# A hand-written order and a planner: moving one unit's outputs, the load gates and the order of a stage in a fused attention and feed-forward kernel

## The chip, the cores and the metric

The kernel runs on one core of one Trainium2 chip. The metric is the device time of one execution in microseconds (us). The engines are named as in the profile: PE is TensorE (matmuls), PEld its weight loads, DVE is VectorE, ACT is ScalarE, POOL is GpSimd, SP is SyncE, which here only issues transfers.

## The reference, cut to what matters

A linear attention with decay over 4 batches, 8 heads, 768 positions and head size 64, followed by a feed-forward layer with a "snake" activation:

```python
for b in range(nb):                      # 12 blocks of 64 positions
    intra = (qb @ kb.T * Dmask) @ vb     # per batch and head
    inter = (qb * lam_pow) @ kv_state
    out[block b] = intra + inter
    kv_state = lam_block * kv_state + kb_dec.T @ vb
x = out as [3072 tokens, 512]
h = x @ w_in                             # 512 -> 2048
g = h + sin(alpha * h) ** 2 / (alpha + 1e-9)
return g @ w_out                         # 2048 -> 512
```

## The kernel before

**Attention.** The work is cut into 24 units: unit s holds a batch, a pair of 128-position blocks and half of the heads. `load_x(s)` issues three transfers on SP's queue (q, k and v of the unit, 256 KB each). `prep(s)` calls `scale_block(s)`, which writes q times a power of lambda, k cast to bf16, and v times a power of lambda (L498 for q and v on POOL or DVE, L509 for k on ACT or POOL). `piece_T(s)` transposes q and k: for units below 8 on TensorE into bank 0 with a copy out (L528, L533; "T4" in the order), from unit 8 on by a transposing transfer on SP's queue (L518), which `prep(s)` issues. `run(S, O, Z)` is one block of small matmuls (L603): S stands for the scores of a unit, O for the outputs of a unit whose masked scores are ready, Z for the sum of k times v that the next unit needs. After it come the masking of the scores (M, L623, DVE), the cast of the sum (Z, L632), the copy of the outputs into xT (E, L642, ACT or DVE), and for outputs of units from 4 on a wipe of half of two banks (L649, DVE). `piece_G(s, s - 1)` ("G5") is one run with scores and sum of unit s, and with the outputs of unit s - 1 unless those have already been computed by a run of their own ("O4", "O7", "O8", which enter `ahead`). Inside a run that has matmuls both before and after the scores, the last part waits on a semaphore for the first.

**Feed-forward.** The 3072 tokens are 6 chunks of 512; chunk c needs the outputs of units 4c to 4c + 3. The first layer of a chunk has 16 column blocks m. `unit_A` does one m for all 512 tokens (four matmuls of 512 columns, L673), `unit_A2` two m for half of the tokens (eight matmuls of 256 columns, L707). Behind them ACT computes the sine (t, L683 or L717), ACT or POOL the square (u, L687, L688, L721, L722), DVE the sum into gT (L690, L725). Only then is the bank free. `unit_B` is a quarter of the second layer for 128 tokens (four matmuls, L738), every fourth followed by a copy (L751) and a store (L753). Chunk 0's first layer uses six banks, chunk 1's three (5, 6, 7) in turn.

**Weights.** The quarter 0 of w_in comes over SP (ws, cast at L437), the other three quarters of w_in (w1_1 to w1_3) and the four of w_out (w2_0 to w2_3) over POOL's queue, cast on the way. The string `LOADS` gives their order together with units 4 to 9 (written v_4 to v_9, although all three transfers are meant): "w2_1:v_4" is not issued before v of unit 4 has landed.

**What sets the order.** Every step is first entered into a list with an estimated duration, its reads, its writes and a place. `_Plan._order` then lays the list out in time by those estimates, and each engine's queue is emitted in that order, with semaphore waits for what the estimates got wrong. TensorE may take any of its next 40 entries: the one with the lowest place among those that start within 0.3 us of the earliest. SP keeps the order of the text. ACT, DVE and POOL take what starts first, and where several could start, the lowest place; `lead` moves a place ahead by so many entries. Some steps may go to either of two engines, by the estimates.

**The stage that the change touches.** After units 0 to 3 the kernel does chunk 0's first layer (eight A2, eight A). Then comes the string `FIRST`: "B" is the next quarter of the second layer, "0" and "1" are the next A2 of chunk 1 for its first and second half of tokens, "A" a `unit_A` of chunk 1, P, T, G, O and L are prep, transposes, a run with scores, a run of outputs, and loads of the unit named. The stores of chunk 0 are issued on SP where the sixteenth B stands. After `FIRST` a loop over chunks 2 to 5 alternates A and B with the remaining units, and the last B follow alone.

Of the kernel before, what the change touches and what calls it, by code (L numbers as in the profile page):

```python
# [270 lines left out]
def bass_lightning_attn__then__act_snake_kernel(  # L271
# [10 lines left out]
    B, H, S, D = q.shape  # L282
# [23 lines left out]
    with es:  # L306
# [48 lines left out]
        def _(_unused_eng):  # L355
            P = _Plan(
                {"PE": nc.tensor, "ACT": nc.scalar, "DVE": nc.vector, "POOL": nc.gpsimd, "SP": nc.sync},
                new_sem,
            )
# [20 lines left out]
            def hop(kind, s, eng, *rest, **more):  # L380

                lead, P.lead = P.lead, P.lead + RANK.get((kind, s), 0)
                e = HEAD.get((kind, s))
                o = op(e, rest[0], COST[kind][e], *rest[2:], **more) if e else op(eng, *rest, **more)
                o.port = kind in ("q", "k", "v", "ws") or (kind, s) == ("alpha", 2)
                P.lead = lead
                return o
# [5 lines left out]
            def bank(i):  # L393
                return ("bank", i)
# [39 lines left out]
            def cast_w1_first():  # L434
                for lo in (0, 256):
                    hop("ws", lo // 256, "DVE",
                       lambda e, lo=lo: (e.copy if e is nc.scalar else e.tensor_copy)(  # L437
                           w1[:, :, lo:lo + 256], ws[:, :, lo:lo + 256]), 0.7, [("ws", lo)], [("w1", lo // 256)])
# [99 lines left out]
            def run(S=None, O=None, Z=None, b0=3, obs=None, parted=False, after=(), us=(0, 1)):  # L538
# [3 lines left out]
                first, free, then = [], [], []  # L542
# [49 lines left out]
                busy = {(a, b): 0 for a in range(2) for b in range(2)}  # L592
                first, early, then = [dealt(g, busy) for g in (first, free, then)]
# [16 lines left out]
                reads, writes = [], []  # L610
# [6 lines left out]
                for r, z in sums:  # L617
                    reads += [("k2", z % R2), ("v2", z % R2)]
                    writes += [bank(ZB[z % 2])] * (bank(ZB[z % 2]) not in writes)
                hop("P", (S, O, Z), "PE", mm, (0.17 if first and then else 0.15) + max(busy.values()) / 1000, reads, writes, after=after)  # L620
                lead, P_.lead = P_.lead, -20
                if S is not None:
                    hop("M", (S, us), "DVE", lambda e: e.tensor_tensor(  # L623
# [29 lines left out]
            def piece_G(s, t):  # L653
                run(S=s, O=t, Z=s)
# [107 lines left out]
            def prep(s, more=True):  # L762
                if s < NBLK:
                    if more and 4 < s < NBLK - 2:
                        load_x(s + 2)
                    P.lead = -20 if 3 < s < 15 else 0
                    P.lead = 0 if 3 < s < 15 else 0
                    P.lead = 20 if 3 < s < 15 else 0
                    scale_block(s)
                    P.lead = 0  # L770
                    P.lead = 0
                    P.lead = 0
                    if s >= TD:
                        piece_T(s, None)
# [25 lines left out]
            run(O=3, obs=(6, 7), parted=True)  # L800
            load_w1_first()
            cast_w1_first()
            LOADS = "w1_1:q_3 w1_2:k_3 w1_3:q_3 v_4 w2_0:q_3 w2_1:v_4 v_5:w1_2 w2_2:w1_2 v_6:ws_1 v_7:w1_3 v_8:ws_0 w2_3:w1_2 v_9:w1_3"
            for x in LOADS.split():
                x, _, gate = x.partition(":")
                x, i = x.split("_")
# [32 lines left out]
            def attend(kind, s):  # L839
# [3 lines left out]
                else:  # L843
                    if 12 < s < NBLK:
# [1 line left out]
                    piece_G(s if s < NBLK else None, s - 1 if s > 4 and s - 1 not in ahead else None)  # L846
                P.lead = 0

            FIRST = ("P4 B P5 P6 B T4 B P7 G4 L10 B B B O4 B T5 T6 B "
# [3 lines left out]
            AT = {2: (5, 8, 12, 13), 3: (2, 6, 10, 13), 4: (2, 6, 10, 13)}  # L853
            at = [0, 0]
            ahead = set()
            for x in FIRST.split():
                if x in "01":
# [8 lines left out]
                elif x[0] == "O":  # L866
                    s = int(x[1:])
# [66 lines left out]
```

## Time and profile before

| | |
|---|---|
| three runs | 214.80, 214.88, 215.81 us; median 214.88 |
| the profiled execution, its own time | 214.99 us |
| its span, first to last instruction | 213.2 us |
| granted TensorE clock | 1.00 in every stretch |
| DMA share, 17.6 to 80.1 us | 1.08 to 1.23 (16 engines, overlapping packets count twice) |
| read from HBM, written | 27.27 MB, 6.29 MB |

A row of the timeline has start, length, engine, line, operation, what it writes and reads, and a count where neighbours were merged; in brackets the engine's idle time ahead of it and what ended it. A matmul's length includes its way through the array, so lengths of neighbours overlap, and distances between starts say what a piece costs. A row of a group (line, engine, operation) has the count, then the total busy time and the mean in ns, then idle time ahead.

### The profile page before, as it was taken

The numbers are of one execution on the slowest core, as the hardware profiler recorded it, in microseconds if no ns is written. First come the engines' busy times: TensorE is split into PE (matmuls) and PEld (weight loads), VectorE is DVE, ScalarE is ACT, GpSimd is POOL, SyncE is SP. The second block draws the span as 40 slices with busy tenths as digits, with TensorE's granted clock in tenths as the row PEclk, the third lists the DMA queues.
The fourth block names the chain that finished last, engine by engine and source line by source line (L and its number), as shares of the span: only waits on it lengthen the run. The fifth ranks groups of instructions, "written<-read, shape, count | busy, mean of one in ns | idle before, by whom it ended". The sixth has DMA issues, their size and how long they took to land.

```text
span 213.2 us, 5249 instructions
## 1 busy us (share of the span) xinstructions
PE 202.9 (95%) x2219; PEld 108.8 (51%) x2219; DVE 124.5 (58%) x196; ACT 162.3 (76%) x296; POOL 74.9 (35%) x82
## 2 busy tenths in 40 slices
PE   7577999999999999999999999999999999999995
PEld 3355834556677655455545545445545444444443
DVE  4584589647788896674846557546646544444200
ACT  6487998149998898878978978888888787888421
POOL 3676787167657554884168400000000000000000
PEclk9999999999999999999999999999999999999999
DMA  5999999999999999999999921101101101110122
GB/s 160 291 318 260 207 212 216 270 279 282 189 268 239 267 284 248 203 300 317 228 206 283 177 49 52 49 3 49 52 0 51 52 0 49 51 52 6 43 98 98
DMA packets 63323, 34.43 MB, mean 161 GB/s; under 512 B 18611, under 2 KB 60355, under 8 KB 63299
## 3 DMA queue, kind: packets, MB, share of 16 engines
q1 hardware_dynamic: 56688, 25.24, 52.7%
q0 software_dynamic: 3696, 3.67, 10.3%
q10 hardware_dynamic: 2914, 5.19, 6.6%
q8 instruction: 17, 0.28, 0.6%
q14 instruction: 8, 0.06, 0.1%
HBM read 27.27 MB, written 6.29 MB: 157 GB/s over the span
## 4 chain that ended last, share of the span: by engine, by line
PE 77%; DVE 7%; SPq 4%; ACT 4%; DMA 3%; POOL 3%; issue 1%; ACTq 0%; POOLq 0%
PE bank L738 37%; PE bank L673 27%; PE bank L603 7%; PE bank L707 5%; SPq L397 4%; DMA ws<-in_moe_w_in_dram 3%; DVE gT L725 2%; POOL u L722 2%; ACT t L717 2%; DVE Sm L623 2%; DVE bank L649 1%; PE bank L528 1%; DVE gT L690 1%; DVE xT L642 1%; ACT u L721 0%
## 5 line engine op out<-in xcount | busy, mean ns | idle before, releaser
L738 PE MATMUL bank<-w,gT 128*128 128x512 bf16 (+2 forms) x400 | 95.5, 371 | 0.0
L690 DVE SCALAR_TENSOR_TENSOR gT<-u,rinv,bank 128x512 bf16<-128x512 bf16 x70 | 51.7, 744 | 44.5 <-ACT u L687 40.6
L673 PE MATMUL bank<-xT,w 128*128 128x512 bf16 x280 | 70.7, 379 | 0.1
L683 ACT ACTIVATE t<-bank,alpha 128x512 bf16<-128x512 f32 x70 | 47.7, 688 | 17.4 <-PE bank L673 17.4
L738 PEld LDWEIGHTS bank<-w,gT 128*128 128x128 bf16 x400 | 36.9, 98 | 39.4 <-ACT osb L751 0.9
L673 PEld LDWEIGHTS bank<-xT,w 128*128 128x128 bf16 x280 | 27.1, 98 | 33.1 <-DVE gT L725 1.1
L687 ACT ACTIVATE u<-t 128x512 bf16<-128x512 bf16 x61 | 38.3, 631 | 1.8
L623 DVE TENSOR_TENSOR Sm<-bank,mask 128x1024 bf16<-128x1024 f32 (+1 forms) x25 | 29.3, 1177 | 8.8 <-PE bank L603 8.8
L498 POOL TENSOR_TENSOR qk<-q,Lq 128x512 bf16<-128x512 f32 x24 | 25.3, 1054 | 12.8 <-DMA q<-in_q_dram 10.5
L498 POOL TENSOR_TENSOR v<-v,Lk 128x512 bf16<-128x512 f32 x22 | 22.9, 1042 | 13.3 <-DMA v<-in_v_dram 10.2
L707 PE MATMUL bank<-xT,w 128*128 128x256 bf16 x208 | 25.6, 273 | 1.7 <-ACT w L437 0.5
L725 DVE SCALAR_TENSOR_TENSOR gT<-u,rinv,bank 128x256 bf16<-128x256 bf16 x52 | 21.7, 469 | 7.8 <-POOL u L722 6.3
L717 ACT ACTIVATE t<-bank,alpha 128x256 bf16<-128x256 f32 x52 | 22.2, 473 | 3.7 <-PE bank L707 3.5
L751 ACT COPY osb<-bank 128x512 f32<-128x512 f32 (+2 forms) x25 | 14.0, 562 | 12.0 <-PE bank L738 12.0
L707 PEld LDWEIGHTS bank<-xT,w 128*128 128x128 bf16 x208 | 19.4, 98 | 6.6 <-DVE xT L642 0.9
L509 ACT CAST qk<-k 128x512 bf16<-128x512 f32 x22 | 13.6, 619 | 6.2 <-DMA k<-in_k_dram 6.2
L722 POOL TENSOR_TENSOR u<-t 128x512 bf16<-128x512 bf16 x10 | 10.4, 1040 | 8.9 <-ACT t L717 8.8
L642 ACT CAST xT<-bank 128x512 bf16<-128x512 f32 (+1 forms) x18 | 13.0, 722 | 0.4 <-PE bank L603 0.3
L688 POOL TENSOR_TENSOR u<-t 128x512 bf16<-128x512 bf16 x9 | 9.3, 1039 | 10.0 <-ACT t L683 9.2
L632 ACT CAST Zc<-bank 128x256 bf16<-128x256 f32 x22 | 8.0, 365 | 5.3 <-PE bank L603 5.3
L603 PE MATMUL bank<-qkT,Zc 64*64 64x128 bf16 x160 | 11.4, 228 | 0.5
L649 DVE MEMSET bank<- 128x512 f32 x20 | 9.7, 485 | 3.2 <-ACT xT L642 1.1
(53 smaller groups left out, 111.9 us busy)
## 6 DMA issues: line engine op xcount, KB each, us to landing
q<-in_q_dram SPq DMA_DIRECT2D x24, 256.0 KB, 5.4
k<-in_k_dram SPq DMA_DIRECT2D x24, 256.0 KB, 5.3
v<-in_v_dram SPq DMA_DIRECT2D x24, 256.0 KB, 5.6
out_dram<-osb ACTq DMA_DIRECT2D x19, 256.0 KB, 2.0
w<-in_moe_w_out_dram POOLq DMA_DIRECT2D x4, 512.0 KB, 13.1
w<-in_moe_w_in_dram POOLq DMA_DIRECT2D x3, 512.0 KB, 10.7
ws<-in_moe_w_in_dram SPq DMA_DIRECT2D x2, 512.0 KB, 6.9
out_dram<-osb SPq DMA_DIRECT2D x4, 256.0 KB, 3.5
```

What stands on the lines that cost most here:

```text
L498: return lambda e: e.tensor_tensor(out, bass.AP(x32[x][jl], 0, [[8 * D, 128], [4 * D, 2], [D, 4], [1, D]]), bass.AP(L, (2 * n + g) * 8, [[ ...
L603: ins = e.matmul(d, w, x, start=key not in begun, stop=True, skip_group_check=True)
L623: hop("M", (S, us), "DVE", lambda e: e.tensor_tensor(Sm[S % 2][:, us[0]:us[-1] + 1, :, :].rearrange("p u w i -> p (u w i)").rearrange("p ( ...
L642: hop("E", O if not parted else (O, r0), eng, lambda e, r0=r0, r1=r1, ra=ra, way=way: (e.copy if e is nc.scalar else e.tensor_copy)(bass.A ...
L673: ins = e.matmul(ps[hb][:, c0:c1], w1[:, kc, 128 * m:128 * (m + 1)], xT[x][:, kc, c0:c1], start=(kc == 0 and c0 == lo), stop=(kc == NKC - ...
L683: op("ACT", lambda e: e.activation(t16[ju][:, w], ps[hb][:, w], ACTF.Sin, scale=alpha[:, m:m + 1]), 0.69 * f, [bank(hb), "alpha"], [("t16" ...
L687: lambda e: (e.activation(u16[ju][:, w], t16[ju][:, w], ACTF.Square) if e is nc.scalar else e.tensor_tensor(u16[ju][:, w], t16[ju][:, w], ...
L690: op("DVE", lambda e: e.scalar_tensor_tensor(out=gT[g][:, m, w], in0=u16[ju][:, w], scalar=rinv[:, m:m + 1], in1=ps[hb][:, w], op0=ALU.mul ...
L707: ins = e.matmul(ps[hb][:, 256 * i:256 * i + 256], w1[:, kc, 128 * (m + i):128 * (m + i + 1)], xT[x][:, kc, lo:lo + 256], start=(kc == 0 a ...
L717: op("ACT", lambda e, i=i: e.activation(t16[ju][:, 256 * i:256 * i + 256], ps[hb][:, 256 * i:256 * i + 256], ACTF.Sin, scale=alpha[:, m + ...
L725: op("DVE", lambda e, i=i: e.scalar_tensor_tensor(out=gT[g][:, m + i, lo:lo + 256], in0=u16[ju][:, 256 * i:256 * i + 256], scalar=rinv[:, ...
L738: ins = e.matmul(ps[ob][:, w], gT[g][:, m, 128 * s4:128 * (s4 + 1)], w2[:, m, w], start=(m == 0), stop=(m == NM - 1),)
```

## The change

Five edits, all in what the planner is given:

- the estimated length of a run: 0.17 or 0.15 us plus its matmuls before; now 0.12 for a run with one part, 0.165 where scores stand between the two parts, 0.39 where they don't (O4, O7, O8)
- the lead of `scale_block` for units 4 to 14: from 20 entries ahead to 20 entries back
- `LOADS`: unit 4's loads and w2_0 come first in the text; v_4 is gated on k_3, w2_0 on v_4 (before: q_3), w1_1 on k_3, unit 5 on w1_3 (before: w1_2), units 6 to 9 on other gates, all of which come behind unit 5 on the same queue
- `FIRST`: "O4" is gone, so that G5 computes unit 4's outputs; the rest is ordered anew, with the same count of B, G, P, T and L; the two closing A are one more 0 and one more 1
- in consequence the loads of units 11 and 12 stand one transposing transfer further ahead on SP, and chunk 0's stores behind the loads of units 14 to 16

```diff
-                hop("P", (S, O, Z), "PE", mm, (0.17 if first and then else 0.15) + max(busy.values()) / 1000, reads, writes, after=after)
+                hop("P", (S, O, Z), "PE", mm, (0.12 if not then or not first else 0.165 if early else 0.39) + max(busy.values()) / 1000, reads, writes, after=after)
...
                     P.lead = -20 if 3 < s < 15 else 0
                     P.lead = 0 if 3 < s < 15 else 0
-                    P.lead = 20 if 3 < s < 15 else 0
+                    P.lead = -20 if 3 < s < 15 else 0
                     scale_block(s)
...
-            LOADS = "w1_1:q_3 w1_2:k_3 w1_3:q_3 v_4 w2_0:q_3 w2_1:v_4 v_5:w1_2 w2_2:w1_2 v_6:ws_1 v_7:w1_3 v_8:ws_0 w2_3:w1_2 v_9:w1_3"
+            LOADS = "v_4:k_3 w2_0:v_4 w1_1:k_3 w2_1:v_4 w1_2:q_3 w1_3:q_3 v_5:w1_3 w2_2:w1_2 v_6 v_7:w1_1 v_8:w1_3 w2_3:w1_2 v_9:w2_0"
...
-            FIRST = ("P4 B P5 P6 B T4 B P7 G4 L10 B B B O4 B T5 T6 B "
-                     "P8 B T7 B B B P9 L11 G5 P10 G6 B 0 G7 0 O7 L12 0 "
-                     "0 1 G8 1 O8 B 0 G9 L13 1 1 G10 1 0 1 P11 P12 1 "
-                     "B B G11 P13 0 L14 G12 B L15 L16 B P14 A A")
+            FIRST = ("B P4 P5 P6 B P7 B L10 B T4 T5 G4 B P8 L11 B G5 T6 "
+                     "B P9 B B L12 B G6 T7 P10 B B G7 0 0 0 O7 L13 0 "
+                     "B 0 1 G8 1 O8 1 1 P11 P12 1 G9 B P13 B 1 L14 0 "
+                     "L15 G10 L16 B G11 B G12 0 1 1 P14 B 0")
```

## The prediction

> **What bounds the kernel now.** I read the page's totals and its chain of waits first, then the windows for the stages, then TensorE's timeline for the places where it does not run back to back.
>
> ```profile
> span 213.2 us, 5249 instructions
> PE 202.9 (95%) x2219; PEld 108.8 (51%) x2219; DVE 124.5 (58%) x196; ACT 162.3 (76%) x296; POOL 74.9 (35%) x82
> ...
> PE 77%; DVE 7%; SPq 4%; ACT 4%; DMA 3%; POOL 3%; issue 1%; ACTq 0%; POOLq 0%
> ```
>
> ```profile
> 17.60:34.10 16.50, 15.23 (x120) 9.52 (x121) 10.77 (x23) 14.86 (x33) 11.95 (x13) 1.00 1.23 217
> 34.10:49.30 15.20, 15.13 (x210) 8.11 (x207) 9.83 (x13) 6.57 (x14) 7.78 (x8) 1.00 1.08 258
> 49.30:80.10 30.80, 29.57 (x484) 20.61 (x481) 25.73 (x49) 27.64 (x62) 19.81 (x20) 1.00 1.14 256
> 80.10:197.80 117.70, 117.57 (x1101) 56.99 (x1102) 66.08 (x93) 98.03 (x166) 24.60 (x25) 1.00 0.50 114
> ```
>
> The columns of the second view are the stretch, its length, then busy time of PE, PEld, DVE, ACT and POOL, the granted clock, the DMA share and GB/s. The first row is chunk 0's first layer, the second chunk 0's second layer (twelve B) with units 4 to 6, the third chunk 1's first layer with units 7 to 12, the fourth the steady rest. TensorE holds 77% of the chain. From 80.1 to 197.8 it is busy for 117.57 of 117.70 us, so the change cannot win anything there, and it does not touch that part. What can be won lies ahead of 80.1: work taken off TensorE, or the pieces in which it waits.
>
> A busy matmul includes its pipeline tail, so I take the cost of a piece as the distance from its start to the next piece's start.
>
> ```profile
> 57.53 1.03 PE L738 MATMUL bank<-w,gT 128*128 128x512 bf16 x4
> 58.40 1.04 PE L707 MATMUL bank<-xT,w 128*128 128x256 bf16 x8
> ...
> 63.30 1.03 PE L738 MATMUL bank<-w,gT 128*128 128x512 bf16 x4
> 64.67 0.42 PE L603 MATMUL bank<-qkT 64*64 64x128 bf16 x16 [0.34 <-DVE bank L649]
> ```
>
> The B at 57.53 hands over after 0.87 us; that is its price with nothing in the way. The B at 63.30 hands over after 1.37 us: 0.50 us of waiting, for the wipe of the banks after unit 8's outputs. Three more such places:
>
> ```profile
> 49.34 1.05 PE L707 MATMUL bank<-xT,w 128*128 128x256 bf16 x8
> 50.59 0.42 PE L603 MATMUL bank<-Sm,v 64*64 64x128 bf16 x16 [0.20 <-DVE qkT L533]
> ```
>
> ```profile
> 75.75 1.04 PE L707 MATMUL bank<-xT,w 128*128 128x256 bf16 x8
> 76.96 0.42 PE L603 MATMUL bank<-Sm,v 64*64 64x128 bf16 x16 [0.17 <-DVE bank L649]
> ...
> 77.81 1.05 PE L707 MATMUL bank<-xT,w 128*128 128x256 bf16 x8
> 78.69 1.03 PE L738 MATMUL bank<-w,gT 128*128 128x512 bf16 x4
> 80.16 1.05 PE L707 MATMUL bank<-xT,w 128*128 128x256 bf16 x8 [0.44 <-DVE xT L642]
> ```
>
> The A2 at 77.81 costs 0.88. So 49.34 to 50.59 holds 0.38 of waiting (unit 7's transposes, just issued), 75.75 to 76.96 holds 0.34 (a wipe again) and 78.69 to 80.16 holds 0.60 (unit 11's outputs on their way into xT). With the 0.50 above: **1.8 us in four places**, each one a unit's step that has too little other work between it and the step that it feeds.
>
> **The change part by part.**
>
> *Unit 4's outputs in G5.* Today O4 is a run of its own, and G5 is a run without outputs:
>
> ```profile
> 40.99 0.42 PE L603 MATMUL bank<-Sm,v 64*64 64x128 bf16 x16
> ...
> 41.72 1.90 PE L738 MATMUL bank<-w,gT 128*128 128x512 bf16 x8
> 43.55 0.42 PE L603 MATMUL bank<-qkT 64*64 64x128 bf16 x16
> ...
> 44.02 1.90 PE L738 MATMUL bank<-w,gT 128*128 128x512 bf16 x8
> ...
> 47.16 0.42 PE L603 MATMUL bank<-Sm,v 64*64 64x128 bf16 x16
> ...
> 48.01 1.04 PE L738 MATMUL bank<-w,gT 128*128 128x512 bf16 x4
> ```
>
> O4 costs 41.72 - 40.99 = 0.73, G5 costs 44.02 - 43.55 = 0.47, and a run that holds both (G6) costs 48.01 - 47.16 = 0.85. So the merge takes 0.73 + 0.47 - 0.85 = **0.35 us** off TensorE in a stage where it is busy for 15.13 of 15.20 us; nothing else covers it, so it counts in full. The copy to xT and the wipe stay, one place later.
>
> *The new order of FIRST.* The counts stay: 18 B, G4 to G12, O7, O8, sixteen m of chunk 1. Only the two closing A become one 0 and one 1. What moves: two B stand between T7 and G7 (today only the A2 at 49.34 runs there, and G7 waits for T7), three A2 between O8 and G9 (today one B and one A2), and four A2 and a B behind G12, where today come two A. Those are the places of the 0.38, 0.50, 0.34 and 0.60 us. On paper each gets at least one more piece of 0.87 us, more than the wait. But the planner may take any of TensorE's next 40 operations that it believes ready, so the text is not the order. I take **half, 0.9 us**, with bounds of 1.8 gained and, if the A2 that now stand closer wait in turn, 2.7 lost (worked out under the rivals).
>
> ```profile
> L690 DVE SCALAR_TENSOR_TENSOR gT<-u,rinv,bank 128x512 bf16<-128x512 bf16 x70 | 51.7, 744 | 44.5 <-ACT u L687 40.6
> ...
> L683 ACT ACTIVATE t<-bank,alpha 128x512 bf16<-128x512 f32 x70 | 47.7, 688 | 17.4 <-PE bank L673 17.4
> ...
> L725 DVE SCALAR_TENSOR_TENSOR gT<-u,rinv,bank 128x256 bf16<-128x256 bf16 x52 | 21.7, 469 | 7.8 <-POOL u L722 6.3
> L717 ACT ACTIVATE t<-bank,alpha 128x256 bf16<-128x256 f32 x52 | 22.2, 473 | 3.7 <-PE bank L707 3.5
> ```
>
> Two A as two A2 cost ACT 4 x 0.473 - 2 x 0.688 = 0.52 us more and DVE 4 x 0.469 - 2 x 0.744 = 0.39 more. The third stage has 30.80 - 27.64 = 3.2 us of ACT and 5.1 of DVE left, so I price it at 0; without that cover it would be 0.5.
>
> *Units 4 to 14 scaled later (lead 20 to -20).* It only decides where several operations are ready for one engine. On the chain that the trace follows, scaling stands ahead of the layer's own work twice in the third stage:
>
> ```profile
> 67.07 0.51 ACT qk L509
> ...
> 71.47 1.00 POOL v L498
> ```
>
> Both push back the squares that release banks. They are the means by which the 0.9 above is won, not a further term. The price is that the transposes of units 8 to 10 may come later.
>
> *The loads, in chunk 0's first layer.*
>
> ```profile
> 20.75 0.63 ACT L509 CAST qk<-k 128x512 bf16<-128x512 f32 x1
> ```
>
> ```profile
> 24.57 0.80 POOL L397 DMA_DIRECT2D w<-in_moe_w_out_dram  x1 [1.28 <-DMA v<-in_v_dram]
> 25.39 1.05 POOL L722 TENSOR_TENSOR u<-t 128x512 bf16<-128x512 bf16 x1
> ```
>
> ```profile
> 23.29 3.67 PE L707 MATMUL bank<-xT,w 128*128 128x256 bf16 x32 [0.25 <-DMA w<-in_moe_w_in_dram]
> 26.80 7.53 PE L673 MATMUL bank<-xT,w 128*128 128x512 bf16 x32
> 34.16 1.03 PE L738 MATMUL bank<-w,gT 128*128 128x512 bf16 x4
> ```
>
> POOL's queue now waits with w2_1 for v_4 (1.28 us, to 24.57), and a square is stuck behind it. In the new plan w2_0 waits for v_4 too, so two issues of 0.80 may stand there: up to 0.80 us later. Against that, unit 4's cast at 20.75 can give way. TensorE's loss there is small: the eight A from 26.80 to 34.16 take 7.36 where 8 x 0.865 = 6.92 would do, so 0.44. I take **0** (bounds: 0.44 won, 0.80 lost). w2_0 itself is not late: it queues behind the w1 loads on the same queue and is wanted at 34.16.
>
> *Unit 5's loads, gated on w1_3 in place of w1_2.*
>
> ```profile
> 26.11 0.37 SPq L397 DMA_DIRECT2D q<-in_q_dram  x1
> ```
>
> ```profile
> 39.59 0.61 PE L528 MATMUL bank<-ident,qk 128*128 128x128 bf16 x8
> ```
>
> ```profile
> 41.20 1.04 POOL L498 TENSOR_TENSOR v<-v,Lk 128x512 bf16<-128x512 f32 x1 [5.01 <-DMA v<-in_v_dram]
> ```
>
> w1_1 ended a wait at 23.29 and w1_2 let q5 go at 26.11, so a weight load takes about 2.8 us and w1_3 lands near 28.9 (an estimate from these two rows): unit 5 is asked for 2.8 us later. Its v arrived at 41.20, 15 us after the first issue, because it shared the DMA engines with the four w2 loads (DMA share 1.08 in that stage). The time that SP stays out, the weights use, so I expect v5 less than 1 us later: scaled by 43.2, and G5, today at 43.55, not held. Twelve B of 0.87 are there to stand ahead of it. Price 0; if the whole 2.8 us came through, about 1.5 (rivals).
>
> The Trainium skill, page "DMA: Bandwidth & Descriptors", section "Queues, rings and completion order", says that each DMA engine takes the queues that have work in turn, a packet from each. By it SP's absence is fully given to the weights and the sum stays as above; by a mere shift the sum would be 1.5 us worse. The trace speaks for the rule, with v5's 15 us beside busy weights.
>
> *The real lengths of runs* change only what the planner believes (0.39 for a run of outputs with no scores, 0.165 with). They cost no time themselves.
>
> **Sum.** -0.35 - 0.9 + 0 + 0 = -1.25 us. The span of 213.2 becomes 211.95. The profiled execution took 214.99, 1.79 beside the span, so 213.74; it lies 0.11 above the median of 214.88. Predicted: **213.6 us**, 0.6% faster. A measurement of this kernel can tell about 0.5% (1.07 us) from no change, so 213.8 is the edge.
>
> **The rivals.**
>
> *A2 too close (slower).* From G7 to G9 the new text has ten A2 with one B, the old one six with one. An A2 keeps ACT for 2 x 0.473 + 0.63 where ACT also squares, some 1.5 us, against 0.87 on TensorE: 0.6 lost for each A2 that has nothing beside it; 0.95 and 0.08 lost where POOL squares. Eight bare A2, half of each kind: 4 x 0.60 + 4 x 0.08 = 2.7. With the merge 214.88 - 0.35 + 2.7 = 217.2. It decides once the planner finds no B ready in its 40. For it: ACT is busy for 27.64 of 30.80 us there. Against: chunk 0's last four B need nothing of chunk 1.
>
> *Unit 5 late (slower).* If v5 lands 2.8 us later, at 44.0, G5 runs at 45.1; the B and the transposes cover about half, G6 and the first A2 come some 1.5 us later, and the waits in the third stage are not won: 214.88 - 0.35 + 1.5 = 216.0. Against: the shared engines, above.
>
> *Waits that move.* ACT at 90% in the third stage makes new waits where the old ones go: only the merge is left, 214.5. For it: ACT gets 0.52 us more.
>
> *The order hardly changes.* The planner's window of 40 gives back much the old order: 214.88 - 0.35 = 214.5.
>
> *The second POOL issue costs its 0.80.* 213.6 + 0.8 = 214.4.
>
> **How the numbers follow.** Forecast, with its larger gains: 0.47. Waits that move 0.12, same order 0.08, the second issue 0.08: 0.28 within 0.5%. A2 too close 0.15, unit 5 late 0.10: 0.25 slower. The best case is 214.88 - 0.35 - 1.8 - 0.44 = 212.3; I put the lower end a little under it, 212.0, since O7 and O8 may be better placed too. The upper end takes in unit 5 late and part of the crowded A2: 216.4. About 0.08 is left out below and 0.10 above.
>
> **What would show it right or wrong.** One run of 0.85 us for G5 and none for O4: the merge. TensorE without waits ahead of G7 and G9 and after G12, and the third stage ending over 1 us earlier: the order. If TensorE's B are used up before G5, unit 5 was late. If the third stage shows ACT over 92% busy and A2 waiting for banks, they stand too close. A span of chunk 0's first layer longer than 16.5 us: POOL's second issue.

## The result and the profile after

The changed kernel takes 217.17 us (median of four runs, 216.72 to 218.53), the kernel before 214.84 beside it: a ratio of 1.0109, interval 1.0059 to 1.0158. It is **1.1% slower**, where I forecast 0.6% faster, and outside my range. Ratios here compare only executions within 1.5% of the fastest of their kernel, and an execution whose inputs land late (below) can fall on either side of that line. The profiled execution took 218.53, with a span of 216.8; three of the four runs lie between 216.72 and 217.31, so the profile shows some 1.3 us more than is usual, and I had to find out first in which stage those lie.

The page's totals and chain of the changed kernel, then its windows. The first two rows are cut at the same events as before (first A2, first B, first A2 of chunk 1). The third is not: with the new order it ends ahead of chunk 2's first A and holds 556 matmuls, where before it held 484, so I don't compare its length:

```profile
span 216.8 us, 5261 instructions
PE 203.0 (94%) x2226; PEld 109.3 (50%) x2226; DVE 124.7 (58%) x198; ACT 162.2 (75%) x298; POOL 75.0 (35%) x82
...
PE 78%; DMA 8%; SPq 4%; DVE 4%; ACT 3%; POOL 1%; issue 1%; ACTq 0%
```

```profile
17.90:36.40 18.50, 15.32 (x120) 9.54 (x121) 11.07 (x23) 15.21 (x33) 12.39 (x13) 1.00 1.07 184
36.40:52.50 16.10, 15.08 (x209) 8.24 (x207) 8.63 (x11) 7.36 (x16) 8.22 (x8) 1.00 1.18 267
52.50:85.30 32.80, 32.13 (x556) 23.51 (x556) 27.69 (x55) 29.91 (x69) 22.17 (x23) 1.00 1.10 246
```

TensorE's busy time is the same (203.0 against 202.9). The first layer takes 18.50 us instead of 16.50 with the same matmuls, and DMA has 8% of the chain instead of 3%. The second stage holds 15.08 us of work in 16.10, where before it was 15.13 in 15.20: TensorE now waits there for 1.0 us.

To compare kernels I measure from the first B (the first row of L738): what comes behind it repeats closely in executions that differ by a microsecond and more ahead of it. The changed kernel took 180.36 and 180.38 us in two profiles; four variants with the same TensorE order up to G7 (e1, e3, e4, e10) reach G7 0.24 us later, all of it lost in the first 3.6 us. So I read nothing into differences under 0.3 us.

| from the first B, us | to G5 | G5 to G6 | to G7 | G7 to the end | to the end |
|---|---|---|---|---|---|
| before | 9.39 | 3.61 | 16.42 | 162.63 | 179.05 |
| after | 10.42 | 3.71 | 17.54 | 162.81 | 180.36 |

So of the 3.54 us between the two profiled executions 1.31 lie behind the first B (1.3 to 1.6 in all profiles of this order), and 2.25 ahead of it (first B at 36.41 against 34.16). The medians differ by 2.33, so about 1.0 of them is left for the first layer.

**Behind the first B.** TensorE's timeline of the changed kernel around G5 (46.82), G6 (50.53), the first A2 (52.55) and G7 (53.95); the columns are start, length, engine, line, what it does, and in brackets the idle time ahead and what ended it:

```profile
46.82 0.42 PE L603 MATMUL bank<-Sm,v 64*64 64x128 bf16 x16
...
47.67 1.04 PE L738 MATMUL bank<-w,gT 128*128 128x512 bf16 x4
48.55 0.61 PE L528 MATMUL bank<-ident,qk 128*128 128x128 bf16 x8
48.99 1.03 PE L738 MATMUL bank<-w,gT 128*128 128x512 bf16 x4
50.53 0.42 PE L603 MATMUL bank<-Sm,v 64*64 64x128 bf16 x16 [0.51 <-DVE bank L649]
...
51.38 0.62 PE L528 MATMUL bank<-ident,qk 128*128 128x128 bf16 x8
52.55 1.05 PE L707 MATMUL bank<-xT,w 128*128 128x256 bf16 x8 [0.55 <-ACT xT L642]
53.95 0.42 PE L603 MATMUL bank<-Sm,v 64*64 64x128 bf16 x16 [0.36 <-DVE bank L649]
```

G5 with unit 4's outputs costs 47.67 - 46.82 = 0.85: that part of the sum is exact. But the B at 48.99 hands over after 1.54 instead of 0.87, 0.67 lost to the wipe behind unit 4's outputs. The transposes at 51.38 hand over after 1.17 where 0.45 is usual, 0.72 lost to xT. The A2 at 52.55 hands over after 1.40 instead of 0.87, 0.53 lost to the next wipe. That is 1.92 us, where before only G7 waited (0.37). VectorE shows the first of them: G6 needs the copy of unit 6's transposes and the wipe, and the wipe stands second:

```profile
49.19 0.69 DVE L533 COPY qkT<-bank 128x1024 bf16<-128x1024 bf16 x1 [0.19 <-PE bank L528]
49.99 0.48 DVE L649 MEMSET bank<- 128x512 f32 x1
```

The difference of 1.55, less the merge's 0.35, gives 1.20; measured from the first B to G7 are 1.12.

**From G7 on** the waits that I aimed at did go (0.50 and 0.34 fell to 0.26 or less, the 0.60 ahead of chunk 2's third A2 is gone), and one came:

```profile
85.35 1.90 PE L673 MATMUL bank<-xT,w 128*128 128x512 bf16 x8
88.06 1.04 PE L673 MATMUL bank<-xT,w 128*128 128x512 bf16 x4 [0.81 <-DVE gT L725]
```

Two A from 85.35 should hand over at 87.09; the third starts at 88.06, 0.97 later. With several waits of 0.14 to 0.26 that before did not have, the whole is 0.18 longer (162.81 against 162.63).

### The profile page after: what moved, and what is told of

Same layout as the page of the kernel before. It is cut to its first block, busy times and chain, and to the rows that moved or that the text cites. A ratio compares the mean times of both kernels' runs of the same rounds, so it can differ in the third digit from the quotient of the medians.

```text
span 216.8 us, 5261 instructions
## 1 busy us (share of the span) xinstructions
PE 203.0 (94%) x2226; PEld 109.3 (50%) x2226; DVE 124.7 (58%) x198; ACT 162.2 (75%) x298; POOL 75.0 (35%) x82
## 4 chain that ended last, share of the span: by engine, by line
PE 78%; DMA 8%; SPq 4%; DVE 4%; ACT 3%; POOL 1%; issue 1%; ACTq 0%
PE bank L738 38%; PE bank L673 26%; PE bank L603 7%; PE bank L707 7%; DMA v<-in_v_dram 5%; SPq L397 4%; DMA k<-in_k_dram 3%; DVE gT L725 2%; DVE Sm L623 1%; ACT osb L751 1%; ACT t L717 1%; ACT u L721 1%; POOL w L397 1%; POOL u L722 0%; ACT qk L509 0%
## 5 line engine op out<-in xcount | busy, mean ns | idle before, releaser
L738 PE MATMUL bank<-w,gT 128*128 128x512 bf16 (+2 forms) x400 | 94.8, 371 | 0.0
L690 DVE SCALAR_TENSOR_TENSOR gT<-u,rinv,bank 128x512 bf16<-128x512 bf16 x68 | 50.2, 744 | 46.7 <-ACT u L687 41.9
L673 PE MATMUL bank<-xT,w 128*128 128x512 bf16 x272 | 68.9, 379 | 2.7 <-DVE gT L725 2.7
L683 ACT ACTIVATE t<-bank,alpha 128x512 bf16<-128x512 f32 x68 | 46.4, 688 | 17.5 <-PE bank L673 17.5
L738 PEld LDWEIGHTS bank<-w,gT 128*128 128x128 bf16 x400 | 36.8, 98 | 40.6 <-ACT osb L751 1.6
L673 PEld LDWEIGHTS bank<-xT,w 128*128 128x128 bf16 x272 | 26.2, 98 | 35.0 <-DVE gT L725 4.4
L687 ACT ACTIVATE u<-t 128x512 bf16<-128x512 bf16 x58 | 36.5, 630 | 1.8
L707 PE MATMUL bank<-xT,w 128*128 128x256 bf16 x224 | 27.2, 273 | 3.0 <-DVE w L437 1.3
L725 DVE SCALAR_TENSOR_TENSOR gT<-u,rinv,bank 128x256 bf16<-128x256 bf16 x56 | 23.6, 472 | 8.8 <-POOL u L722 6.6
L717 ACT ACTIVATE t<-bank,alpha 128x256 bf16<-128x256 f32 x56 | 23.7, 479 | 4.4 <-PE bank L707 4.3
L707 PEld LDWEIGHTS bank<-xT,w 128*128 128x128 bf16 x224 | 21.0, 98 | 8.1 <-DVE w L437 1.4
L721 ACT ACTIVATE u<-t 128x512 bf16<-128x512 bf16 x19 | 12.3, 647 | 0.2
L603 PEld LDWEIGHTS bank<-Sm,v 64*64 64x64 bf16 x384 | 6.3, 106 | 10.0 <-issue 5.5
```

Of the source, the lines that this page charges most:

```text
L603: ins = e.matmul(d, w, x, start=key not in begun, stop=True, skip_group_check=True)
L673: ins = e.matmul(ps[hb][:, c0:c1], w1[:, kc, 128 * m:128 * (m + 1)], xT[x][:, kc, c0:c1], start=(kc == 0 and c0 == lo), stop=(kc == NKC - ...
L683: op("ACT", lambda e: e.activation(t16[ju][:, w], ps[hb][:, w], ACTF.Sin, scale=alpha[:, m:m + 1]), 0.69 * f, [bank(hb), "alpha"], [("t16" ...
L687: lambda e: (e.activation(u16[ju][:, w], t16[ju][:, w], ACTF.Square) if e is nc.scalar else e.tensor_tensor(u16[ju][:, w], t16[ju][:, w], ...
L690: op("DVE", lambda e: e.scalar_tensor_tensor(out=gT[g][:, m, w], in0=u16[ju][:, w], scalar=rinv[:, m:m + 1], in1=ps[hb][:, w], op0=ALU.mul ...
L707: ins = e.matmul(ps[hb][:, 256 * i:256 * i + 256], w1[:, kc, 128 * (m + i):128 * (m + i + 1)], xT[x][:, kc, lo:lo + 256], start=(kc == 0 a ...
```

## Theories, and what each run told

After the comparison I had four theories for parts of the loss. **Landing**: unit 4's k and v land late, and two weight issues, both waiting for v on POOL's queue, hold up the squares. **Unit 5 late**: the loads of unit 5, asked for later, delay G5 and use up the B. **The merge**: unit 4's copy and wipe now stand between G5 and G6. **Waits that move**: the order takes waits away in one place and gets them back in another, because an engine beside TensorE (ScalarE's squares, or VectorE's queue, in order) cannot go faster. A "plan unchanged" edit takes out or replaces a dependence only after the order has been laid out, so every engine keeps its order. Ratios are to the kernel before on the same chip; a row without one had a single run.

| run | median (range; runs) | ratio, interval | first B | to G7 | G7 to end | first B to end |
|---|---|---|---|---|---|---|
| e1 | 218.03 (216.48-218.76; 4) | 1.0129, 1.0047-1.0211 | 34.13 | 17.79 | 162.81 | 180.60 |
| e2 | 216.53 (214.72-219.58; 10) | 1.0033, 0.9985-1.0081 | 34.29 | 16.42 | 162.64 | 179.07 |
| e3 | 216.47 (216.13-218.16; 10) | 1.0071, 1.0024-1.0118 | 34.32 | 17.78 | 162.83 | 180.61 |
| e4 | 217.42 (216.17-218.42; 4) | 1.0107, 1.0025-1.0189 | 33.82 | 17.78 | 162.82 | 180.60 |
| e5 | 217.58 (216.51-219.46; 4) | 1.0111, 1.0065-1.0156 | 37.50 | 17.39 | 162.82 | 180.22 |
| e6 | 216.08 (214.98-219.53; 10) | 1.0039, 1.0016-1.0062 | 37.43 | 16.95 | 163.37 | 180.32 |
| e7 | 217.41 (216.61-217.85; 4) | 1.0115, 1.0077-1.0153 | 34.06 | 17.98 | 163.77 | 181.75 |
| e8 | 216.17 (215.88-218.90; 10) | 1.0094, 1.0056-1.0132 | 34.01 | 16.49 | 163.76 | 180.25 |
| e9 | 217.74 (215.87-220.74; 9) | 1.0111, 1.0075-1.0147 | 33.15 | 17.22 | 163.76 | 180.97 |
| e10 | 220.03 | | 36.81 | 17.79 | 163.69 | 181.48 |
| e11 | 220.34 | | 37.68 | 16.51 | 164.39 | 180.91 |
| e12 | 216.05 (215.57-218.99; 10) | 1.0062, 1.0028-1.0095 | 34.14 | 16.21 | 163.47 | 179.68 |
| e13 | 219.28 | | 37.48 | 17.55 | 162.51 | 180.06 |
| e14 | 217.56 | | 36.73 | 16.44 | 162.64 | 179.08 |
| e15 | 218.96 (216.85-220.50; 6) | 1.0149, 1.0062-1.0235 | 37.43 | 17.55 | 162.84 | 180.38 |
| e16 | 214.79 (214.07-216.91; 12) | 0.9992, 0.9945-1.0038 | 35.87 | 16.35 | 162.62 | 178.97 |
| e17 | 219.63 | | 37.55 | 17.56 | 162.77 | 180.32 |
| e18 | 217.99 | | 35.51 | 16.52 | 164.20 | 180.72 |

### The first layer

e1, the changed kernel with unit 4's loads not gated; e2, the kernel before with that gate; both with the order of every engine unchanged:

```diff
-            LOADS = "v_4:k_3 w2_0:v_4 ...
+            LOADS = "v_4 w2_0:v_4 ...
```

```diff
-            LOADS = "w1_1:q_3 w1_2:k_3 w1_3:q_3 v_4 w2_0:q_3 ...
+            LOADS = "w1_1:q_3 w1_2:k_3 w1_3:q_3 v_4:k_3 w2_0:q_3 ...
```

> The changed kernel with unit 4's loads let go without the gate on k of unit 3; every engine's order stays the same, only SP's wait is gone. Theory 1 (the gate on unit 4's loads lets the w1 loads go ahead of k and v of unit 4, which land 2.2 us later, and ACT's cast of k and POOL's w2 issues hold up the sines and squares behind them): v of unit 4 lands near 24.3 instead of 26.6, chunk 0's first layer ends about 2 us earlier, the time is 214.9 to 215.5. Theory 2 (two w2 issues stand behind v of unit 4 on POOL): at most 0.5 won, 216.7 or more. Theory 3 (unit 5's loads come too late): 217, no change.

> The kernel before with only the gate on k of unit 3 for unit 4's loads; every engine's order stays the same. Theory 1: 1.5 to 2.3 us slower, 216.4 to 217.2. Theories 2 and 3: no change, 214.7 to 215.2.

e3, the changed kernel with its plan unchanged, where w2_0 and w2_1 no longer wait for unit 4's v; e16, the kernel before with the same for its w2_1; e15, the changed kernel once more, on the chip of e16:

```diff
-            for d in sorted(o.deps, key=place.get, reverse=True):
+            for d in sorted((o.deps - o.soft) | o.extra, key=place.get, reverse=True):
...
-            hc = [0]
+            hc = [0]; [setattr(last["w2", i], "soft", {last["v", 4]}) for i in range(2)]
```

> The changed kernel, same order and same plan, but w2_0 and w2_1 are issued on POOL without waiting for v of unit 4. Theory 2: POOL's squares come up to 2.5 us earlier and the time is 215.2 to 215.8. Theory 1: ACT's cast of k of unit 4 still holds the sines, so under half of that: 216.2 to 217. Theory 3: no change.

> The changed kernel once more, for a closer time. The later part is 1.3 to 1.55 us longer than before, whatever the run. If chunk 0's first layer is as long as before in a usual run: 216.0 to 216.4, with 214.6 for the kernel before. If two w2 issues behind v of unit 4 on POOL cost in most runs: 216.8 to 217.4.

> The kernel before, same order, but POOL issues w2_1 without waiting for v of unit 4. If POOL's wait of 1.28 us there delays the squares and through them the A of chunk 0: 0.3 to 0.5 us won, 214.2 to 214.5 where the kernel before has 214.7. If not: no change.

In the changed kernel's profile ScalarE and POOL wait for unit 4 like this (two views):

```profile
22.92 0.62 ACT L509 CAST qk<-k 128x512 bf16<-128x512 f32 x1 [1.83 <-DMA k<-in_k_dram]
23.45 1.56 ACT L717 ACTIVATE t<-bank,alpha 128x256 bf16<-128x256 f32 x4
```

```profile
24.36 1.04 POOL L722 TENSOR_TENSOR u<-t 128x512 bf16<-128x512 bf16 x1 [2.15 <-ACT t L717]
26.84 1.55 POOL L397 DMA_DIRECT2D w<-in_moe_w_out_dram  x2 [1.45 <-DMA v<-in_v_dram]
28.41 1.06 POOL L722 TENSOR_TENSOR u<-t 128x512 bf16<-128x512 bf16 x1
```

The cast of k stands ahead of four sines that have their input, and the issues stand ahead of a square. In the prediction's rows the cast ran at 20.75 and POOL went on at 24.57. The landing times of the DMA records settle what the first B follows:

| run | k asked | k landed | v landed | first B | first B less v |
|---|---|---|---|---|---|
| before | 13.03 | 20.68 | 24.28 | 34.16 | 9.88 |
| e2 | 13.96 | 20.79 | 24.40 | 34.29 | 9.89 |
| after | 14.08 | 22.90 | 26.56 | 36.41 | 9.85 |
| e15 | 14.07 | 23.60 | 27.59 | 37.43 | 9.84 |
| e6 | 13.15 | 23.93 | 27.54 | 37.43 | 9.89 |
| e14 | 12.42 | 23.22 | 26.84 | 36.73 | 9.89 |
| e1 | 13.11 | 20.24 | 21.76 | 34.13 | 12.37 |
| e16 | 12.21 | 23.20 | 26.91 | 35.87 | 8.96 |

With POOL's queue held by v, the first B comes 9.84 to 9.89 us after v lands, with one issue behind the wait (before, e2, e6, e14) as with two (after, e15). **So the second issue of 0.80 cost nothing**; the landing is what counts, as long as v lands at about 24 or later. Where it lands earlier something else holds the first B (12.37 in e1, 12.01 in e12), and e10, with v at 25.37, has 11.44: its granted clock was 0.50 from 21 to 25 us, but e15, with 0.61 there, keeps to 9.84, so that the clock is the reason is not shown. Without the wait (e16) it is 0.9 less. The landing itself varies from run to run, both in kernels with unit 4's gate (after and e15 late, e2 early) and in those without it (e6, e14 and e16 late, before and e1 early). In the late ones of the table k lands 3.6 to 3.7 us after q and within 1 us of w1_1 (22.90 and 22.69 after), in the early ones 0.7 to 1.8 us after q and 2 us or more ahead of w1_1. The other runs are not all of one kind or the other: e3 has 2.48 us from q to k, e18 2.84.

That leaves the 1.0 us of the medians. e2 puts the gate at 0.7 us with an interval from -0.3 to 1.7; e1, without the gate, won nothing (1.0129). In e3 the ratio of 1.0071 comes to 1.5 us, no more than its 1.56 behind the first B, and e16 won nothing on the kernel before. e15 missed both times that I had named: 218.96, with a ratio of 1.0149 that leaves 1.9 us for the first layer on that chip. Its profiled execution landed late. The first layer's share is thus within the spread of the landing, and what in the change makes the late landing commoner, if anything does, **stays open**.

### Unit 5's loads

e4, the changed kernel with its plan unchanged and unit 5's loads behind w1_2 as before; e7, the same gate, planned anew; e8, the old `LOADS` throughout, planned anew:

```diff
-            hc = [0]
+            hc = [0]; [(setattr(last[x, 5], "soft", {last["w1", 3]}), setattr(last[x, 5], "extra", {last["w1", 2]})) for x in "qkv"]
```

```diff
-   ... w1_3:q_3 v_5:w1_3 w2_2:w1_2 ...
+   ... w1_3:q_3 v_5:w1_2 w2_2:w1_2 ...
```

```diff
-            LOADS = "v_4:k_3 w2_0:v_4 w1_1:k_3 ...
+            LOADS = "w1_1:q_3 w1_2:k_3 w1_3:q_3 v_4 w2_0:q_3 ...
```

> The changed kernel, same order and same plan, but unit 5's loads wait for w1_2 as before, not for w1_3. Theory 3: units 5 to 8 land 2.5 us earlier and the waits ahead of G6, T7 and the first A2 (1.9 us) go: 215.2 to 215.8. Theory 1: the loss of chunk 0's first layer stays, 216.7 or more.

> The changed kernel with unit 5 gated on w1_2 as before, and planned anew with it. Theory 5: eight B ahead of G5, the stretch from the first B to G7 falls by 1 us or more, the time to 215 to 215.8. Theory 4 alone: under 0.4 us.

> The changed kernel with the whole old text of the loads, planned anew. If the gates are at the root of both losses (POOL's and ACT's waits in chunk 0's first layer, the late G5): first layer and stretch as before the change or shorter, 213.9 to 214.8. If the new order or the merge is at fault: 215.5 or more.

In e4 unit 5's v lands at 41.71, 7.89 us behind the first B, instead of 44.77 and 8.36 in the changed kernel, and not one of the three waits moves: G5 stands 10.65 us behind the first B, and the end is at 180.60 as in e1 and e3. So G5 is late because the order puts ten B ahead of it, not because its data are. e8 shows what set that order: with the old `LOADS` v lands 7.91 us behind the first B, as in e4, but eight B stand ahead of G5, G5 comes at 9.07 and the way to G7 takes 16.49, as before. The planner believed in the later landing, and by that belief spent its B. But e8 gives nearly all of it back behind G7 (163.76 against 162.81), so unit 5's delay sets where the loss lies, and hardly its size. e7 is a miss for the simple cure: the planner now puts G6 4.85 us behind G5, and the kernel is the longest of all behind the first B (181.75).

### Unit 6's cast behind a copy

Unit 6's k is cast on ScalarE behind an output copy that waits for a B, with ScalarE idle for 3.58 us ahead of the copy (46.93, the cast at 47.41). e5 is the changed kernel with that cast first, with the line that names the cast left out here:

```diff
-                op("ACT", lambda e: e.copy(osb[jo][:, w], ps[ob][:, w]), 0.6, [bank(ob)], [("osb", jo)])
+                op("ACT", lambda e: e.copy(osb[jo][:, w], ps[ob][:, w]), 0.6, [bank(ob)], [("osb", jo)], after=[last["cast", 6]] if (c, s4) == (0, 0) else [])
```

> The changed kernel with one more dependency: ACT's first copy of a finished second-layer bank (t0 of chunk 0) comes behind the cast of k of unit 6, which it preceded; a few neighbours on PE, DVE and ACT shift with it. From the first B to G7 it took 16.4 us before the change and 17.5 to 17.8 in the runs of the changed kernel and its variants. Theory 4 (in ACT's order unit 6's cast stands behind a copy that waits for a B, so T6, G6 and G7 are late): G6 follows G5 after about 2.7 instead of 3.7 us, the stretch falls to 16.8 or less, the time by 0.7 to 1.2 us. Theory 5 (G5 itself stands too late on TensorE, with ten B ahead of it instead of eight, since the plan believes unit 5 late): the stretch stays above 17.3.

G6 comes 0.16 us earlier (3.55 behind G5), and so does the end. Taking the cast out of its place behind 3.58 us of idle time, on an engine off the path, was worth 0.15, less than the spread of 0.24 above.

### The merge alone

e6, the kernel before with "O4" taken out of `FIRST`, nothing else:

```diff
-            FIRST = ("P4 B P5 P6 B T4 B P7 G4 L10 B B B O4 B T5 T6 B "
+            FIRST = ("P4 B P5 P6 B T4 B P7 G4 L10 B B B B T5 T6 B "
```

> The kernel before with only O4 taken out of the order, so that G5 computes unit 4's outputs. The prediction's step: 0.35 us less TensorE work, 214.1 to 214.6 beside 214.9. Rival: the copy and the wipe of unit 4's outputs now stand between G5 and G6, so the stretch from the first B to G7 grows by 0.5 to 1.3 us instead and the time with it, 215.3 to 216.

The end is 1.27 us later from the first B, and the ratio of 1.0039 excludes a gain. Three timelines of e6 around the place, TensorE, ScalarE and VectorE:

```profile
51.69 0.62 PE L528 MATMUL bank<-ident,qk 128*128 128x128 bf16 x8
53.64 0.81 PE L738 MATMUL bank<-w,gT 128*128 128x512 bf16 x3 [1.33 <-ACT qkT L533]
```

```profile
51.80 0.37 ACT L632 CAST Zc<-bank 128x256 bf16<-128x256 f32 x1 [0.26 <-PE bank L603]
52.35 1.01 ACT L533 COPY qkT<-bank 128x1024 bf16<-128x1024 bf16 x1 [0.18 <-PE bank L528]
```

```profile
51.80 1.23 DVE L623 TENSOR_TENSOR Sm<-bank,mask 128x1024 bf16<-128x1024 f32 x1 [1.02 <-PE bank L603]
52.94 0.72 DVE L642 CAST xT<-bank 128x512 bf16<-128x512 f32 x1
53.84 0.48 DVE L649 MEMSET bank<- 128x512 f32 x1 [0.18 <-DVE xT L642]
```

The loss is not in the merged run (46.92 to 47.77 on the chain, 0.85 again), nor in the wipe behind it: the last B ahead of G6 starts at 49.88 and G6 at 50.84, 0.96 later, with no wait. It is in what the planner did with the shorter run. Nine B stand ahead of G5 instead of eight, so the twelfth B stands ahead of G6, and unit 7's transposes follow G6 at once (51.69), where before the twelfth B stood between. G6 leaves a mask, a copy to xT and a wipe on VectorE, 1.23 + 0.72 + 0.48 us; so the transposes' copy goes to ScalarE and takes 1.01, the thirteenth B needs the bank that it frees, and TensorE loses 1.50. To G7 the loss is 0.53; the other 0.74 lie behind it, and I did not trace them. The profiled execution of e6 took 219.53 where the median is 216.08, so 1.27 is the figure of one profile; the interval of the ratio, 0.3 to 1.3 us, takes it in.

### The order alone, and the order with O4 back

e11, the kernel before with the new `FIRST` but "O4" in it (its line below is against the new `FIRST`); e9, the changed kernel with "O4" back; e10, the changed kernel with two closing A; e12, the changed kernel with the old `LOADS`, "O4" and two A:

```diff
-  e9, e11, e12:  ... G4 B P8 L11 B G5 T6 ...
+                 ... G4 B P8 L11 O4 B G5 T6 ...
-  e10, e12:      ... G12 0 1 1 P14 B 0")
+                 ... G12 0 1 P14 B A A")
```

> The kernel before with the new order, but O4 kept as a run of its own; old loads, old lengths, old lead. By the prediction's step for the order alone: 0.9 us won, the first B to the end 178.2 (179.05 before). If the waits only move: 178.9 to 179.3. If the end of the new order costs its 0.97 us: 179.5 to 180.

> The changed kernel with O4 as a run of its own again, ahead of G5; all else as changed. From the first B to the end it took 179.05 us before the change and 180.4 to 180.6 in the changed kernel, whatever its start. Theory 6 (the merge is what costs: unit 4's copy and wipe now stand between G5 and G6, and the twelve B are used up while G6, T7 and the first A2 wait 1.9 us): those waits fall under 0.8 us and the first B to the end takes 179.2 to 179.7. Theory 5 (G5 late because the plan believes unit 5 late): the waits stay, 180.3 or more.

> The changed kernel with two A in the place of the last 0 and 1 at the end of the order. Theory 7 (A2 crowd behind G12, their banks come free late, and a later A waits 0.97 us for one): that wait falls under 0.3 us and the first B to the end takes 179.5 to 179.9. If the wait comes from DVE's queue whatever stands there: no change, 180.4 to 180.6.

> The changed kernel with three things undone: the old loads, O4 on its own, two A at the end. What is left of the change is the order between G6 and G12, the lengths and the lead. If those are sound, the first layer is as before (16.5 us), the first B to the end takes 178.2 to 179.1 and the time is 214.0 to 214.9; if they too cost, 215.3 or more.

**The order alone loses 1.86 us** behind the first B (180.91 against 179.05), where I had it gain 0.9. Up to G7 it costs 0.09; then TensorE loses 0.56, 1.00, 0.36 and 1.05 us between 41 and 52 us after the first B, 2.97 in all. The rest of the way is thus 1.2 us shorter than before: old waits went, for more than the 0.9 that I took, and the new ones cost over twice that. The second and the fourth of them:

```profile
81.41 1.05 PE L707 MATMUL bank<-xT,w 128*128 128x256 bf16 x8
83.29 1.04 PE L738 MATMUL bank<-w,gT 128*128 128x512 bf16 x4 [0.83 <-DVE gT L725]
...
88.06 1.04 PE L673 MATMUL bank<-xT,w 128*128 128x512 bf16 x4 [0.30 <-DVE gT L725]
89.98 1.04 PE L673 MATMUL bank<-xT,w 128*128 128x512 bf16 x4 [0.88 <-DVE gT L725]
```

In e9 the waits ahead of G6 and of the first A2 are gone; 0.37 is left ahead of G7, 0.40 is new ahead of a unit's transposes, and the way to G7 is 0.32 shorter than in the changed kernel. But from G7 on it is 0.95 longer, and the end is 0.61 later (180.97 against 180.36): **in the new order, putting O4 back does not help**, and the merge is no loss there. Each variant is laid out anew, so the parts do not add: alone the merge costs 1.27 and the order 1.86, and the whole change costs 1.31. In e9 consecutive A behind chunk 1 wait twice, which the changed kernel does once:

```profile
82.37 1.03 PE L673 MATMUL bank<-xT,w 128*128 128x512 bf16 x4
84.03 1.04 PE L673 MATMUL bank<-xT,w 128*128 128x512 bf16 x4 [0.63 <-DVE gT L725]
85.52 1.04 PE L673 MATMUL bank<-xT,w 128*128 128x512 bf16 x4 [0.46 <-DVE gT L725]
```

e8 has two such waits too (0.91 and 0.62 us lost; 0.79 and 0.63 in e9), e10 is no better for its two A (181.48), and e12, the best of these orders, has 179.68 and a ratio of 1.0062: still slower than before. What e8 and e9 gained ahead of G7 came back where A follow one another. e12 differs from e11 by the lengths, the lead and the two closing A, and ends 1.23 us earlier; which of them does that was not separated, and in the changed kernel two A alone made it worse (e10).

### What sets the late waits

e13 and e14, the changed kernel and the kernel before with ScalarE's squares of chunk 1 computing one column only (the rest of these squares is left out); e17, the changed kernel, and e18, e11's kernel, with unit 12's mask on an eighth of its columns (the rest of that masking is left out). The orders are unchanged. The first cut below is made for A2 and, in the same way, for A; the mask's two other operands are cut like the one shown:

```diff
...
-                   lambda e: (e.activation(u16[ju][:, :], t16[ju][:, :], ACTF.Square) if e is nc.scalar else
+                   lambda e: (e.activation(u16[ju][:, 0:1] if c == 1 else u16[ju][:, :], t16[ju][:, 0:1] if c == 1 else t16[ju][:, :], ACTF.Square) if e is nc.scalar else
```

```diff
...
-                        bass.AP(mask, 0, [[256, 128], [0, 2 * len(us)], [1, 256]]), ALU.mult),
+                        bass.AP(mask, 0, [[256, 128], [0, 2 * len(us)], [1, 32 if S == 12 else 256]]), ALU.mult),
```

> The changed kernel, same order on every engine, but where ACT squares for chunk 1 it does one column only; that part of the square is left out, about 0.43 us less of ACT for each of some eight squares. From the first B to the end it took 180.4 to 180.6. Theory 8 (from the first A2 to the steady part ACT's work is the bound, and PE's waits only move along): the wait of 0.97 us goes, and 0.8 to 1.2 us of the stretch with it: 179.3 to 179.8; the waits ahead of G6, T7 and the first A2 stay. Rival (DVE's queue, with the masks ahead of the sums, holds the banks): 180.2 or more.

> The kernel before with the same cut, same order. From the first B to the end it took 179.05. Theory 8: waits of 0.5 to 1.1 us go, 178.0 to 178.5. Rival (masks and wipes on DVE): 178.8 or more.

> The changed kernel with every instruction in its place; VectorE's mask of unit 12's scores covers an eighth of its columns (the rest of the masking is left out), so the 1.22 us at 86.01 shrink to an estimated 0.2 to 0.3. Theory (VectorE's own order sets the wait: the mask stands ahead of the two sums that the A at 88.06 needs): that wait of 0.97 us falls to under 0.2, and the time from the first B to the end falls from 180.4 to about 179.5. Rival (ScalarE's squares set it, and the mask is only the last thing before it): the wait stays at 0.8 or more, and the time from the first B to the end stays at 180.2 or more.

> The new order alone with unit 4's outputs left as a run of their own, and the same mask of unit 12 cut to an eighth (the rest of that masking is left out). Theory (VectorE's order): of the last of its four waits, 1.05 us where the mask at 87.92 stands ahead of two sums, at least 0.8 goes, and the time from the first B to the end falls from 180.9 to about 180.0, leaving the waits of 0.56, 1.00 and 0.36 as they are. Rival (ScalarE): VectorE had idled 1.32 us for ScalarE's square just ahead of that mask, so the wait stays, and the time from the first B to the end stays at 180.7 or more.

**ScalarE's squares are not the bound.** The kernel before doesn't feel their absence (179.08 against 179.05), with twelve of them at about 0.2 us instead of 0.63 the changed one gains 0.3, and its late wait stays: in e13 two A start at 86.12 and the third at 88.82, again 0.96 late.

For VectorE the chain of waits of the changed kernel speaks, ahead of the A at 88.06:

```profile
83.69 0.85 ACT t L717 x2
84.53 0.02 issue
84.56 0.64 ACT u L721
85.20 0.02 issue
85.22 0.87 DVE gT L725 x2
86.09 1.13 DVE Sm L623
87.23 0.79 DVE gT L725 x2
```

A unit's mask stands for 1.13 us between the sums that release banks. I took it for unit 12's, and e17 showed me wrong; VectorE's rows of e17:

```profile
82.13 0.29 DVE L623 TENSOR_TENSOR Sm<-bank,mask 128x128 bf16<-128x128 f32 x1 [0.17 <-PE bank L603]
...
87.18 1.22 DVE L623 TENSOR_TENSOR Sm<-bank,mask 128x1024 bf16<-128x1024 f32 x1
```

The short mask is five microseconds too early; the one in the chain follows G13 and is whole, so the wait of 1 us stays, and e17 decides nothing on it. In e18 the short mask does stand between two sums, ahead of e11's wait of 1.00. VectorE and TensorE there:

```profile
79.07 0.48 DVE L725 SCALAR_TENSOR_TENSOR gT<-u,rinv,bank 128x256 bf16<-128x256 bf16 x1 [0.40 <-ACT u L721]
79.47 0.28 DVE L623 TENSOR_TENSOR Sm<-bank,mask 128x128 bf16<-128x128 f32 x1
79.67 0.47 DVE L725 SCALAR_TENSOR_TENSOR gT<-u,rinv,bank 128x256 bf16<-128x256 bf16 x1
```

```profile
80.42 0.81 PE L738 MATMUL bank<-w,gT 128*128 128x512 bf16 x3
81.07 1.04 PE L707 MATMUL bank<-xT,w 128*128 128x256 bf16 x8
82.28 1.05 PE L707 MATMUL bank<-xT,w 128*128 128x256 bf16 x8 [0.17 <-DVE gT L725]
83.63 1.04 PE L673 MATMUL bank<-xT,w 128*128 128x512 bf16 x4 [0.30 <-DVE gT L725]
...
87.62 0.60 PE L673 MATMUL bank<-xT,w 128*128 128x512 bf16 x2 [1.16 <-DVE gT L725]
```

The wait of 1.00 falls to 0.29 or less: 0.7 us gone with 0.94 us of VectorE's queue. But new waits of 0.33 and 0.47 follow at the next two pieces, the last grows from 1.05 to 1.33, and the end moves by 0.19 (180.72 against 180.91), within the spread named above. **So the mask did hold that wait, and the wait was worth almost nothing.** Which step of the ring of three banks (matmul, sine, square, sum) then limits is open: neither the squares nor this mask alone. The mask behind G13 shortened was not tried.

## Why the prediction was wrong, point by point

- *What bounds the kernel.* Right from G16 on: from there to the end it takes 109.33 to 109.36 us in every kernel that I ran. But I drew the line at 80.1, which is 45.9 us behind the first B, and wrote that the change does not touch what comes after. The wait of 0.97 in the changed kernel ends 51.65 us behind the first B, and 1.41 of e11's 2.97 lie behind that line too.
- *The merge, -0.35.* **This step failed.** The run's 0.85 was exact. But "nothing else covers it, so it counts in full" took the order around the run as fixed, and the copy and the wipe, "one place later", got no price. Alone, the merge made the planner put a ninth B ahead of G5; none was left between G6 and unit 7's transposes, and -0.35 became +1.27. In the changed kernel the wipe cost 0.67 ahead of G6. In e6 and e8, merged too, G6 waits for nothing, so that price belongs to the order, not to the merge as such.
- *The order of FIRST, -0.9 with bounds of -1.8 and +2.7.* **This step failed too, in sign**: +1.86 alone. The waits aimed at did shrink, by about 1.2, but I counted the four places that get a piece put between, and not the places from which those pieces were taken: 2.97 us of new waits. Behind G12 I compared four A2 and a B with "two A", where the old text has two A and two B. The rival "waits that move" named the mechanism; its price was too low, for I let it fall to no gain, where it is a loss.
- *Scaling later.* Not tried by itself; priced at nothing as a term of its own.
- *The second POOL issue, 0 (rival: +0.80).* Right: 9.84 to 9.89 us from landing to first B with one issue or two. The sign that I had named for it, a first layer longer than 16.5 us, came (18.50) with another cause. What I lacked was that the landing of v itself varies, from 21.8 to 27.6 us in the table above.
- *Unit 5's loads, 0 (rival: "unit 5 late", 216.0).* **Wrong, by another way than the rival's.** The sign that I named, B used up ahead of G5, came nearly: ten B stood ahead of G5 instead of eight, all twelve were used up ahead of G6, and the first A2 came 0.96 us later, counted from the first B (16.14 against 15.18). But it was the planner's belief, not the landing (e4, e8). Its v landed 8.36 us behind the first B instead of 6.97, 1.4 later where I expected less than 1.
- *The Trainium skill*, "DMA: Bandwidth & Descriptors", section "Queues, rings and completion order": each DMA engine takes the queues in turn, by packets. By it SP's absence goes to the weights, and v5 is hardly later. The trace agrees in part, with 1.4 us and not 2.8, though w2_0 had moved too. By equal turns alone k of unit 4 and w1_1, asked within 0.04 us of each other, should fare alike in each run; they landed 0.2 us apart in the changed kernel and 2.0 apart in e2 (20.79 and 22.81). What decides that, no run here shows.
- *A2 too close.* ACT is busy for 29.91 of 32.80 us in the third row, 91%, close to the 92% that I had named as its sign, and A, though not A2, wait 0.97 for a bank; but e13 and e14 show that ACT's squares don't set the time. Its sines were not tried.
- *The real lengths.* Not run apart; they change the order together with the rest, and e12 beside e11 leaves room for a gain by them.

The sum of the three terms priced at -0.35, -0.9 and 0 was to give -1.25; the kernel has +1.31 behind the first B and about +1.0 ahead of it in the median, the latter not assigned.

## What to carry to other kernels

A step merged into another saves what the trace shows of its matmuls, but only if the order around it holds. Look at the order that the planner makes of it, count what is left to stand between the later steps, and list what each engine has to do between the merged run and the next reader of its banks. A wait that an order takes away counts only if the pieces that fill it had somewhere spare to come from; cut the releasing step alone, as e18 did, and see whether the end moves before reordering for it. Measure from an event behind the part that varies (here the first B), and differences above 0.3 us can be read here from single profiles whose totals differ by 3.

## What I had not expected of the hardware

Executions of one kernel differ by up to 5 us (e2: 214.72 to 219.58). Between profiles of one order most of the difference lies ahead of the first B: unit 4's k lands 0.7 to 2.8 us after its q or 3.6 to 3.7 us after it, beside a weight load asked for within 1.7 us of it, and where POOL waits for it the first B follows v. Behind the first B the same order gave 180.36, 180.38 (after, e15) and 179.05, 179.07 (before, e2). Only one execution of each run was profiled, so that this explains the whole 5 us is not shown.
